# A decode block with attention over 65,536 keys: key and value chunks loaded in turn, a maximum for each chunk, one combination at the end

## The chip, the cores and the metric

The kernel runs on one core of one Trainium2 chip. The metric is the device time of one execution in microseconds (us), given as the median of several runs, with the lowest and the highest. Shorter is better. The profile is of one execution; where the record gives both, its span is about 1.8 us shorter than the time of the same run.

The engines are called as the profile calls them: PE is TensorE (matmuls), PEld its weight loads, DVE is VectorE, ACT is ScalarE, POOL is GpSimd, SP is SyncE, which here issues the loads. A load is one large transfer from memory into a buffer on the chip. The profile counts 16 DMA engines, and each load of the two kernels has 16 marks of completion.

## The reference, cut to what matters

One token goes through a block of a transformer. Attention has one query, 32 heads, 4 key/value heads of 65,536 keys with 128 elements each. All inputs are bfloat16.

```python
mod = (silu(c) @ w_mod).reshape(..., 6, 1, 1024)      # 1024 x 6144 weights: shifts, scales, gates
h = layernorm(x) * (1 + ca) + sa
q = h @ wq                                            # 1024 x 4096
p = softmax(q @ k.T * 128 ** -0.5)                    # k_cache: 4 x 65536 x 128, 8 query heads each
o = p @ v                                             # v_cache: the same shape
x = x + ga * (o @ wo)                                 # 4096 x 1024
h = layernorm(x) * (1 + cb) + sb
x = x + gb * ((gelu(h @ w_gate) * (h @ w_up)) @ w_down)   # 1024 x 3584 twice, 3584 x 1024
```

Everything is read once: 185.6 MB, of which 134 MB are keys and values. There is little arithmetic for each byte (the loads of the kernel before take 95.1% of the DMA engines' time, and PE is busy for 67% of the span), so the aim is that the loads never pause.

## The kernel before

All loads go through a ring of nine 2 MB buffers. SP issues a load as soon as the buffer that it goes to has been released by the matmuls that read it. The order of the loads is fixed by a schedule. `("A", g, cc)` is chunk cc of the keys of head group g, `("B", g, cc)` is a chunk of its values. A chunk has 8,192 keys, and a group has 8 chunks.

```python
NBUF = 9
SKEW = 7
...
S = min(SKEW, NCH)                       # NCH = 8 chunks in a group
for cc in range(NCH):
    sched.append(("A", 0, cc))
for g in range(Hkv):
    if g + 1 < Hkv:
        for cc in range(NCH):
            sched.append(("A", g + 1, cc))
            if cc >= S:
                sched.append(("B", g, cc - S))
        for cc in range(NCH - S, NCH):
            sched.append(("B", g, cc))
    else:
        for cc in range(NCH):
            sched.append(("B", g, cc))
```

With `SKEW = 7` this is eight key chunks of a group, then the eight value chunks of the group before, and so on: long runs of one kind. The two kinds differ in their cost. A key chunk is turned by 64 PE transposes into PSUM, copied out in four pieces of 128 x 2048 (three by DVE, 1.22 us each, one by ACT, 1.88 us), multiplied with the query in 64 matmuls, copied out as scores by ACT and reduced to a maximum by DVE. A value chunk costs only 64 matmuls (1.8 us; 128 take 3.58). The exponentials of a group wait for the maximum of the whole group:

```python
def emit_score_consume(g, cc):           # one key chunk
    ...
    dst = s_hm[:, :, cc * CH:(cc + 1) * CH].rearrange("p h n -> p n h")
    ... act.activation(dst, src, ACT.Copy, scale=scale)               # scores: PSUM -> SBUF
    ... dve.tensor_reduce(m_parts[:, :, cc:cc + 1], src3, AX.X, ALU.max)

def emit_group_max_and_exp(g):           # once for eight key chunks
    ... dve.tensor_reduce(m_col[:, :], m_parts[:, :, :], AX.X, ALU.max)
    ...                                  # transpose, reduce, broadcast by PE and DVE
    for h in range(REP):
        ... act.activation(pb[:, h, :], s_hm[:, h, :], ACT.Exp,
                           bias=Mneg[:, hq:hq + 1], accum_out=z_col[:, hq:hq + 1])
```

The matrix-vector products of the weight stages start a new sum for every load and add the partial sums on DVE. The weights of gate and up are read with a step of 56 bytes between elements (`"p k (m b) -> p k b m", b=28`):

```python
ins = pe.matmul(pp[:, jl:jl + 1], jb.view[:, kk, jl * P:(jl + 1) * P],
                rhs_col[:, k0 + kk:k0 + kk + 1], start=(kk == 0), stop=(kk == nk - 1))
...
vd = C_DVE.bump(dve.tensor_tensor(dst, dst, pp[:, 0:nj], ALU.add))
```

Of the kernel before, what the change touches and what calls it, by code (L numbers as in the profile page):

```python
# [3 lines left out]
dt = mybir.dt  # L4
ACT = mybir.ActivationFunctionType
ALU = mybir.AluOpType
AX = mybir.AxisListType

P = 128
SLOT = 8192  # L10
NBUF = 9
CH_MAX = 64
SKEW = 7
# [3 lines left out]
NKT_BANKS = 16  # L17
DMA_ENGINES = ("sync",)


class Ctr:

    def __init__(self, nc, name):
        self.sem = nc.alloc_semaphore(name)
        self.n = 0

    def bump(self, ins, by=1):
        ins.then_inc(self.sem, by)
        self.n += by
        return self.n  # L30


class PoolBuf:
    def __init__(self, pool, view, fill_sem, fill_val, rel_sem):
        self.pool = pool
        self.view = view
        self.fill_sem = fill_sem
        self.fill_val = fill_val
        self.rel_sem = rel_sem

    def wait(self, eng):
        eng.wait_ge(self.fill_sem, self.fill_val)

    def release(self):
        self.pool.pending.append(self.rel_sem)


class Pool:

    def __init__(self, nc, engines, nbuf, elems):  # L50
        self.nc = nc
        self.engines = engines
        self.nbuf = nbuf
        self.bufs = [nc.alloc_sbuf_tensor(f"pool{i}", [P, elems], dt.bfloat16) for i in range(nbuf)]
        self.fill = [nc.alloc_semaphore(f"pfill{i}") for i in range(nbuf)]
        self.rel = [nc.alloc_semaphore(f"prel{i}") for i in range(nbuf)]
        self.nfill = [0] * nbuf
        self.njobs = 0
        self.pending = []

    def load(self, src, view_fn):
        slot = self.njobs % self.nbuf
        eng = self.engines[self.njobs % len(self.engines)]
        self.njobs += 1
        if self.nfill[slot] > 0:
            eng.wait_ge(self.rel[slot], self.nfill[slot])
        view = view_fn(self.bufs[slot][:, :])
        eng.dma_start(view, src).then_inc(self.fill[slot], 16)  # L68
        self.nfill[slot] += 1
        return PoolBuf(self, view, self.fill[slot], 16 * self.nfill[slot], self.rel[slot])  # L70


def bass_adaLN_cond__gqa_block_cached__geglu_ffn__decode_kernel(
# [15 lines left out]
    assert D % P == 0  # L89
# [7 lines left out]
    assert REP * Hkv == HQ and Hkv >= 2  # L97
    F = B_w_gate.shape[1]
    assert F % P == 0
    FD = F // P  # L100
    M6 = w_mod.shape[1]
    assert M6 == 6 * D
    MD = M6 // P
    NKPP = SK // P
    assert NKPP * P == SK
    CH = min(CH_MAX, NKPP)
    assert NKPP % CH == 0 and CH % 8 == 0
    NCH = NKPP // CH
    NTB = CH // 8
    assert SLOT % DH == 0 and CH * DH <= SLOT  # L110
    HW = SLOT // 2
    assert KD % 2 == 0
    assert REP * CH <= 512
    scale = float(DH) ** -0.5
    S = min(SKEW, NCH)

    sp = nc.sync
    pe = nc.tensor
    act = nc.scalar
    dve = nc.vector  # L120
    pool = nc.gpsimd
    dma_engines = [{"sync": nc.sync, "gpsimd": nc.gpsimd, "scalar": nc.scalar}[e] for e in DMA_ENGINES]

    C_PE = Ctr(nc, "c_pe")
    C_DVE = Ctr(nc, "c_dve")
    C_ACT = Ctr(nc, "c_act")
    C_POOL = Ctr(nc, "c_pool")
# [3 lines left out]
    ident = nc.alloc_sbuf_tensor("ident", [P, P], dt.bfloat16)  # L131
    identf = nc.alloc_sbuf_tensor("identf", [P, P], dt.float32)
    onesf = nc.alloc_sbuf_tensor("onesf", [P, P], dt.float32)
    eps_t = nc.alloc_sbuf_tensor("eps_t", [P, 1], dt.float32)
    halfneg = nc.alloc_sbuf_tensor("halfneg", [P, 1], dt.float32)
    x_row = nc.alloc_sbuf_tensor("x_row", [KD, P], dt.bfloat16)
    c_row = nc.alloc_sbuf_tensor("c_row", [KD, P], dt.bfloat16)
    x_col = nc.alloc_sbuf_tensor("x_col", [P, KD], dt.float32)
    sg_col = nc.alloc_sbuf_tensor("sg_col", [P, KD], dt.float32)
    th_col = nc.alloc_sbuf_tensor("th_col", [P, KD], dt.float32)  # L140
    s_col = nc.alloc_sbuf_tensor("s_col", [P, KD], dt.bfloat16)
    mod_sb = nc.alloc_sbuf_tensor("mod_sb", [P, MD], dt.float32)
    q_acc = nc.alloc_sbuf_tensor("q_acc", [P, HQ], dt.float32)
    q_col = nc.alloc_sbuf_tensor("q_col", [P, HQ], dt.bfloat16)
    stats = nc.alloc_sbuf_tensor("stats", [P, 2], dt.float32)
    junk8 = nc.alloc_sbuf_tensor("junk8", [P, KD], dt.float32)
    me2 = nc.alloc_sbuf_tensor("me2", [P, 2], dt.float32)
    msq = nc.alloc_sbuf_tensor("msq", [P, 1], dt.float32)
    var = nc.alloc_sbuf_tensor("var", [P, 1], dt.float32)
    std1 = nc.alloc_sbuf_tensor("std1", [P, 1], dt.float32)  # L150
    rstd = nc.alloc_sbuf_tensor("rstd", [P, 1], dt.float32)
    hn = nc.alloc_sbuf_tensor("hn", [P, KD], dt.float32)
    ht = nc.alloc_sbuf_tensor("ht", [P, KD], dt.float32)
    h_col = nc.alloc_sbuf_tensor("h_col", [P, KD], dt.bfloat16)
    stats2 = nc.alloc_sbuf_tensor("stats2", [P, 2], dt.float32)
    junk8b = nc.alloc_sbuf_tensor("junk8b", [P, KD], dt.float32)
    me22 = nc.alloc_sbuf_tensor("me22", [P, 2], dt.float32)
    msq2 = nc.alloc_sbuf_tensor("msq2", [P, 1], dt.float32)
    var2 = nc.alloc_sbuf_tensor("var2", [P, 1], dt.float32)
    std2 = nc.alloc_sbuf_tensor("std2", [P, 1], dt.float32)  # L160
    rstd2 = nc.alloc_sbuf_tensor("rstd2", [P, 1], dt.float32)
    attn_acc = nc.alloc_sbuf_tensor("attn_acc", [P, KD], dt.float32)
    x1_col = nc.alloc_sbuf_tensor("x1_col", [P, KD], dt.float32)
    t_att = nc.alloc_sbuf_tensor("t_att", [P, KD], dt.float32)
    hn2 = nc.alloc_sbuf_tensor("hn2", [P, KD], dt.float32)
    ht2 = nc.alloc_sbuf_tensor("ht2", [P, KD], dt.float32)
    h2_col = nc.alloc_sbuf_tensor("h2_col", [P, KD], dt.bfloat16)
    kt_sb = nc.alloc_sbuf_tensor("kt_sb", [P, NKT_BANKS, 8, DH], dt.bfloat16)
    s_hm = nc.alloc_sbuf_tensor("s_hm", [P, REP, NKPP], dt.float32)
    p_hm = nc.alloc_sbuf_tensor("p_hm", [P, REP, NKPP], dt.bfloat16)  # L170
    m_parts = nc.alloc_sbuf_tensor("m_parts", [P, REP, NCH], dt.float32)
    m_col = nc.alloc_sbuf_tensor("m_col", [P, REP], dt.float32)
    z_col = nc.alloc_sbuf_tensor("z_col", [P, HQ], dt.float32)
    mg8 = nc.alloc_sbuf_tensor("mg8", [REP, 1], dt.float32)
    md8 = nc.alloc_sbuf_tensor("md8", [REP, REP], dt.float32)
    Mneg = nc.alloc_sbuf_tensor("Mneg", [P, HQ], dt.float32)
    rz = nc.alloc_sbuf_tensor("rz", [P, REP], dt.float32)
    o_sb = nc.alloc_sbuf_tensor("o_sb", [P, HQ], dt.bfloat16)
    o_pk = nc.alloc_sbuf_tensor("o_pk", [P, HQ], dt.bfloat16)
    QW = P // HQ  # L180
    assert QW * HQ == P and HQ == DH // QW
    LPAD = P - QW
    Lext = nc.alloc_sbuf_tensor("Lext", [P, P + LPAD], dt.bfloat16)
    Mmod = nc.alloc_sbuf_tensor("Mmod", [P, HQ], dt.bfloat16)
    Rmat = nc.alloc_sbuf_tensor("Rmat", [P, HQ, HQ], dt.bfloat16)
    g_acc = nc.alloc_sbuf_tensor("g_acc", [P, FD], dt.float32)
    u_acc = nc.alloc_sbuf_tensor("u_acc", [P, FD], dt.float32)
    t1 = nc.alloc_sbuf_tensor("t1", [P, FD], dt.float32)
    t2 = nc.alloc_sbuf_tensor("t2", [P, FD], dt.float32)
    t3 = nc.alloc_sbuf_tensor("t3", [P, FD], dt.float32)  # L190
    th = nc.alloc_sbuf_tensor("th", [P, FD], dt.float32)
    t4 = nc.alloc_sbuf_tensor("t4", [P, FD], dt.float32)
    u_col = nc.alloc_sbuf_tensor("u_col", [P, FD], dt.bfloat16)
    dn_acc = nc.alloc_sbuf_tensor("dn_acc", [P, KD], dt.float32)
    t_dn = nc.alloc_sbuf_tensor("t_dn", [P, KD], dt.float32)
    y_col = nc.alloc_sbuf_tensor("y_col", [P, KD], dt.float32)
    y_row = nc.alloc_sbuf_tensor("y_row", [KD, P], dt.bfloat16)

    kt_ps = nc.alloc_psum_tensor("kt_ps", [P, 4 * 1024], dt.bfloat16)
    sc_ps = nc.alloc_psum_tensor("sc_ps", [P, 2 * 512], dt.float32)  # L200
    b6 = nc.alloc_psum_tensor("b6", [P, 512], dt.float32)
    b7 = nc.alloc_psum_tensor("b7", [P, 512], dt.float32)
    PP = [sc_ps[:, 0:512], sc_ps[:, 512:1024]]

    B6_CT, B6_XT, B6_TOT, B6_MBC, B6_TOT2 = 0, 8, 16, 128, 144
    B7_OT, B7_ZBC, B7_PK = 0, HQ, 64
    assert HQ + REP <= 64 and B7_PK + max(HQ, FD) <= 512
    kt_fp = kt_ps[:, :].bitcast(dt.float32)
    KT4 = [kt_fp[:, i * 512:(i + 1) * 512] for i in range(4)]
# [3 lines left out]
    def peI(ins, bump=False):  # L213
        if bump:
            return C_PE.bump(ins)
# [601 lines left out]
```

## Time and profile before

| | before |
|---|---|
| time, median of 3 | 466.35 us (466.33 to 467.19) |
| span of the profiled execution | 467.1 us |
| share of 16 DMA engines' time taken by the loads | 95.1% |
| best rate of a slice | 434 GB/s |
| lowest slices inside the stream | 324, 333 and 307 GB/s |

The page divides the span into 40 slices of 11.7 us. These are its rows for PE and DMA busy time (in tenths; 9 is 90% or more) and for the bytes moved, and its lines of the DMA queues (packets, MB, share of the time of 16 engines).

```profile
PE   1344378778687785668877847778785545649963
...
DMA  7999999999999989999998899999789999999992
GB/s 303 422 425 427 430 432 428 426 427 428 428 431 429 406 324 425 429 429 429 421 366 333 348 429 428 431 429 365 307 331 406 434 428 425 422 421 423 430 430 98
...
q1 hardware_dynamic: 15856, 185.61, 95.1%
q8 instruction: 61, 1.00, 0.8%
```

Queue 1 carries the loads. The rate is 420 to 434 GB/s wherever nothing disturbs it, but there are three dips, the deepest slices of which lie near 170, 250 and 335 us (the 15th, 22nd and 29th slice). No slice of this page is above 434 GB/s. (Windows of 10 us read up to 438; a packet counts whole in the window in which it starts.) So the kernel is bound by its loads, and what can be gained is the dips and the two ends. Queue 8 has 61 packets of 16 KB each that the kernel's code does not ask for: they are fetches of the kernel's own instructions.

The dips come from the order of the loads. The timeline of PE in a run of key chunks, in three steps of the cycle (start us, us, line and operation, count, and in brackets the idle time before and what ended it; L506 are transposes, L549 scores):

```profile
107.26 1.95 PE L506 MATMUL kt_ps<-ident,pool 128*128 128x128 bf16 x32
110.59 2.20 PE L506 MATMUL kt_ps<-ident,pool 128*128 128x128 bf16 x32 [1.38 <-DVE kt_sb L531]
112.63 1.74 PE L549 MATMUL sc_ps<-q_col,kt_sb 128*128 128x8 bf16 x64
114.23 1.95 PE L506 MATMUL kt_ps<-ident,pool 128*128 128x128 bf16 x32
```

A key chunk takes 6.97 us (from 107.26 to 114.23), with PE held up by the copies out of PSUM (`kt_sb`, L531). A 2 MB load takes 4.9 us at the full rate. So PE falls behind by 2 us in each key chunk, sixteen of them in a row at the start (groups 0 and 1) and eight in each later run. In the end the nine buffers are full, and SP has no free buffer to load into (its longest wait for one is 11.0 us). These are PE's two costliest waits of the whole kernel (line, cause, total us, number, longest):

```profile
PE b L626 <- issue: 40.3, 14, 6.1
PE kt_ps L506 <- DVE kt_sb L531: 36.9, 31, 1.6
```

The second is the copies. The first belongs to the runs of values, in which PE is quicker than the loads.

```profile
384.97 3.58 PE L626 MATMUL b<-p_hm,pool 128*128 128x8 bf16 x128 [2.02 <-issue]
391.17 3.58 PE L626 MATMUL b<-p_hm,pool 128*128 128x8 bf16 x128 [2.61 <-issue]
397.36 2.73 PE L626 MATMUL b<-p_hm,pool 128*128 128x8 bf16 x96 [2.61 <-issue]
```

These matmuls come in blocks of 128 every 6.2 us, with idle time before each that the profile puts down to "issue": PE waited for nothing that the profile shows. The loads went on at 420 GB/s and more here, so it cost nothing in this last run. Two earlier runs of values (174 to 197 and 260 to 285 us) show the same stops, 8.1 and 11.2 us in all, although every value that they read had landed before they began. There they kept PE from making up its lag before the next run of keys, and so probably deepened the second and third dip; no run tests that.

### The profile page before, as it was taken

The numbers are of one execution on the slowest core, as the hardware profiler recorded it, in microseconds if no ns is written. First come the engines' busy times: TensorE is split into PE (matmuls) and PEld (weight loads), VectorE is DVE, ScalarE is ACT, GpSimd is POOL, SyncE is SP. The second block draws the span as 40 slices with busy tenths as digits, with TensorE's granted clock in tenths as the row PEclk, the third lists the DMA queues.
The fourth block names the chain that finished last, engine by engine and source line by source line (L and its number), as shares of the span: only waits on it lengthen the run. The fifth ranks groups of instructions, "written<-read, shape, count | busy, mean of one in ns | idle before, by whom it ended". The sixth has DMA issues, their size and how long they took to land.

```text
span 467.1 us, 16270 instructions
## 1 busy us (share of the span) xinstructions
PE 314.2 (67%) x7771; PEld 299.3 (64%) x7771; DVE 149.2 (32%) x204; ACT 115.1 (25%) x131; POOL 3.8 (1%) x22
## 2 busy tenths in 40 slices
PE   1344378778687785668877847778785545649963
PEld 1334377767686785668867747668685445649962
DVE  0001055665556550045575103455640000110010
ACT  1000014334463440027434200744350040000000
POOL 2000000000000000000000000000000000000000
PEclk9999999999799995568999756899985555555555
DMA  7999999999999989999998899999789999999992
GB/s 303 422 425 427 430 432 428 426 427 428 428 431 429 406 324 425 429 429 429 421 366 333 348 429 428 431 429 365 307 331 406 434 428 425 422 421 423 430 430 98
DMA packets 15922, 186.65 MB, mean 400 GB/s; under 512 B 1520, under 2 KB 1520, under 8 KB 4592
## 3 DMA queue, kind: packets, MB, share of 16 engines
q1 hardware_dynamic: 15856, 185.61, 95.1%
q8 instruction: 61, 1.00, 0.8%
q14 instruction: 5, 0.04, 0.0%
HBM read 185.60 MB, written 0.00 MB: 397 GB/s over the span
## 4 chain that ended last, share of the span: by engine, by line
issue 81%; DMA 13%; PE 3%; SPq 2%; DVE 1%; POOLq 0%; POOL 0%
DMA pool<-in_B_w_down_dram 7%; DMA pool<-in_w_mod_dram 6%; PE kt_ps L417 2%; SPq L68 1%; PE kt_ps L399 0%; PE sc_ps L348 0%; PE b L438 0%; POOLq L782 0%; POOL rstd L450 0%; PE b L774 0%; SPq L251 0%; DVE hn L453 0%; DVE y_row L776 0%; SPq L252 0%; DVE dn_acc L388 0%
## 5 line engine op out<-in xcount | busy, mean ns | idle before, releaser
L506 PE MATMUL kt_ps<-ident,pool 128*128 128x128 bf16 x2048 | 140.9, 229 | 43.8 <-DVE kt_sb L531 36.9
L506 PEld LDWEIGHTS kt_ps<-ident,pool 128*128 128x128 bf16 x2048 | 126.4, 104 | 54.0 <-DVE kt_sb L531 47.4
L531 DVE COPY kt_sb<-kt_ps 128x2048 bf16<-128x2048 bf16 x96 | 114.5, 1218 | 19.6 <-PE kt_ps L506 18.7
L529 ACT ACTIVATE kt_sb<-kt_ps 128x2048 bf16<-128x2048 bf16 x32 | 60.1, 1877 | 228.5 <-PE kt_ps L506 228.5
L626 PE MATMUL b<-p_hm,pool 128*128 128x8 bf16 x2048 | 57.3, 175 | 40.3 <-issue 40.3
L626 PEld LDWEIGHTS b<-p_hm,pool 128*128 128x128 bf16 x2048 | 56.0, 102 | 41.4 <-issue 41.3
L549 PE MATMUL sc_ps<-q_col,kt_sb 128*128 128x8 bf16 x2048 | 55.7, 166 | 0.0
L549 PEld LDWEIGHTS sc_ps<-q_col,kt_sb 128*128 128x128 bf16 x2048 | 54.5, 96 | 0.0
L574 DVE TENSOR_REDUCE m_parts<-s_hm 128x8 f32<-128x512 f32 x32 | 22.0, 688 | 87.1 <-ACT s_hm L570 87.1
L570 ACT ACTIVATE s_hm<-sc_ps 128x512 f32<-128x512 f32 x32 | 33.7, 1054 | 0.4 <-PE sc_ps L549 0.4
L606 ACT ACTIVATE p_hm<-s_hm,Mneg 128x512 bf16<-128x512 f32 x32 | 22.6, 708 | 32.2 <-DVE Mneg L595 32.2
L651 DVE RECIPROCAL rz<-b 128x8 f32<-128x8 f32 x4 | 0.8, 208 | 93.0 <-PE b L647 93.0
L417 PE MATMUL kt_ps<-h_col,pool 128*128 128x1 bf16 x448 | 28.7, 202 | 2.6 <-DVE h_col L462 2.2
L417 PEld LDWEIGHTS kt_ps<-h_col,pool 128*128 128x128 bf16 x448 | 28.5, 167 | 2.7 <-DVE h_col L462 2.3
L348 PE MATMUL sc_ps<-s_col,pool 128*128 128x1 bf16 x384 | 11.4, 165 | 21.0 <-DMA pool<-in_w_mod_dram 21.0
L348 PEld LDWEIGHTS sc_ps<-s_col,pool 128*128 128x128 bf16 x384 | 10.9, 104 | 21.5 <-issue 18.8
L759 ACT ACTIVATE th<-t 128x28 f32<-128x28 f32 x1 | 0.2, 225 | 71.1 <-DVE t L757 71.1
L348 PE MATMUL sc_ps<-h_col,pool 128*128 128x1 bf16 x256 | 7.4, 165 | 12.0 <-DMA pool<-in_A_wq_dram 12.0
L348 PEld LDWEIGHTS sc_ps<-h_col,pool 128*128 128x128 bf16 x256 | 7.2, 104 | 12.2 <-issue 9.3
L399 PE MATMUL kt_ps<-u_col,pool 128*128 128x1 bf16 x224 | 6.6, 165 | 8.9 <-DMA pool<-in_B_w_down_dram 7.2
L399 PEld LDWEIGHTS kt_ps<-u_col,pool 128*128 128x128 bf16 x224 | 6.3, 104 | 9.3 <-DMA pool<-in_B_w_down_dram 7.5
L399 PE MATMUL kt_ps<-o_pk,pool 128*128 128x1 bf16 x256 | 7.3, 165 | 4.9 <-issue 4.6
(79 smaller groups left out, 49.3 us busy)
## 6 DMA issues: line engine op xcount, KB each, us to landing
pool<-in_A_k_cache_dram SPq DMA_DIRECT2D x32, 2048.0 KB, 24.3
pool<-in_A_v_cache_dram SPq DMA_DIRECT2D x32, 2048.0 KB, 13.2
pool<-in_w_mod_dram SPq DMA_DIRECT2D x4, 2048.0 KB, 17.7
pool<-in_A_wq_dram SPq DMA_DIRECT2D x4, 2048.0 KB, 28.6
pool<-in_A_wo_dram SPq DMA_DIRECT2D x4, 2048.0 KB, 21.6
pool<-in_B_w_gate_dram SPq DMA_DIRECT2D x4, 1792.0 KB, 27.8
pool<-in_B_w_up_dram SPq DMA_DIRECT2D x4, 1792.0 KB, 29.0
pool<-in_B_w_down_dram SPq DMA_DIRECT2D x3, 2048.0 KB, 31.0
```

Of the source, the lines that this page charges most:

```text
L68: eng.dma_start(view, src).then_inc(self.fill[slot], 16)
L348: ins = pe.matmul(pp[:, jl:jl + 1], jb.view[:, kk, jl * P:(jl + 1) * P], rhs_col[:, k0 + kk:k0 + kk + 1], start=(kk == 0), stop=(kk == nk ...
L399: ins = pe.matmul(pp[:, jl:jl + 1], jb.view[:, kk, jl * P:(jl + 1) * P], rhs_col[:, k0 + kk:k0 + kk + 1], start=(kk == 0), stop=(kk == nk ...
L417: ins = pe.matmul(pp[:, b:b + 1], jb.view.rearrange("p k (m b) -> p k b m", b=nb)[:, kk, b, :], rhs_col[:, k0 + kk:k0 + kk + 1], start=(kk ...
L506: ins = pe.transpose(kt_ps[:, phys * 1024 + i * P:phys * 1024 + (i + 1) * P], kb.view[:, n, :], ident[:, :],)
L529: ve = ctr.bump(act.activation(dst, src, ACT.Copy))
L531: ve = ctr.bump(dve.tensor_copy(dst, src))
L549: ins = pe.matmul(sc_ps[:, sbank * 512 + n * REP:sbank * 512 + (n + 1) * REP], kt_sb[:, tb % NKT_BANKS, i, :], q_col[:, g * REP:(g + 1) * ...
L570: state["sc_done"][gc] = C_ACT.bump(act.activation(dst, src, ACT.Copy, scale=scale))
L574: dve.tensor_reduce(m_parts[:, :, cc:cc + 1], src3, AX.X, ALU.max)
L606: act.activation(pb[:, h, :], s_hm[:, h, :], ACT.Exp, bias=Mneg[:, hq:hq + 1], accum_out=z_col[:, hq:hq + 1],)
L626: ins = pe.matmul(b7[:, B7_OT + g * REP:B7_OT + (g + 1) * REP], vb.view[:, n, :], pb[:, :, ncol], start=(cc == 0 and n == 0), stop=(cc == ...
```

## The change

The intent is a steady mixture: one step takes one key chunk and one value chunk, so that PE's work for a step is below the 10 us that its two loads take. That needs the exponentials of a chunk soon after its scores, so each chunk gets a maximum of its own, and the partial outputs, each relative to its own maximum, are kept apart in PSUM columns and weighted once at the end. Along with it, the scores go from PSUM straight into the exponential, matrix-vector products accumulate in PSUM, gate and up are read with a step of 8 bytes, and the removed score buffer makes room for a tenth slot. (The kernel before does not build with ten buffers: it asks for 16,384 bytes more in each partition with 224 left.)

```diff
-NBUF = 9
-SKEW = 7
+NSLOT = 10
+UE = 4
 ... order of the loads
-        for (kind, g, cc) in sched:
-            if kind == "A":
-                jobs_k[(g, cc)] = pool_ring.load(kh[g][:, cc * CH:(cc + 1) * CH, :], view_kv)
-            else:
-                jobs_v[(g, cc)] = pool_ring.load(vh[g][:, cc * CH:(cc + 1) * CH, :], view_kv)
+        for i in range(NC + 2):                        # NC = 32 chunks in all
+            if i < NC:
+                j_k[i] = plan_load(kv_src(kh, i), kv_view)
+            if i >= 2:
+                j_v[i - 2] = plan_load(kv_src(vh, i - 2), kv_view)
 ... exponentials of one chunk, straight from PSUM
+            for h in range(REP):
+                v = AC.done(act.activation(
+                        p_sb[:, i % 3, :, h], scv[:, h, :], ACT.Exp,
+                        bias=mneg[:, i, h:h + 1], scale=scale, accum_out=z_all[:, i, h:h + 1]))
 ... values: every chunk has its own columns
-                    b7[:, B7_OT + g * REP:B7_OT + (g + 1) * REP], vb.view[:, n, :], pb[:, :, ncol],
-                    start=(cc == 0 and n == 0), stop=(cc == NCH - 1 and n == CH - 1),
+                    b7[:, i * REP:(i + 1) * REP], j_v[i].view[:, n, :], p_sb[:, i % 3, n, :],
+                    start=(n == 0), stop=(n == CH - 1),
 ... one step: T transposes, QK scores, PV values (in quarters), MX1/MT/MB the maximum
+        for i in range(NC + 2):
+            on(T, i, 0); on(QK, i - 1, 0); on(T, i, 1); on(QK, i - 1, 1); on(PV, i - 2, 0)
+            on(T, i, 2); on(QK, i - 1, 2); on(QK, i - 1, 3); on(MX1, i - 1); on(PV, i - 2, 1)
+            on(T, i, 3); on(PV, i - 2, 2); on(MT, i - 1); on(PV, i - 2, 3); on(MB, i - 1)
 ... matrix-vector products: only the very first matmul of a bank starts a sum
-                            start=(kk == 0), stop=(kk == nk - 1),
+                            start=first, stop=True, skip_group_check=True,
                         )
+                        first = False
 ... the end: weights of the chunks, exp(own maximum to the group's), applied to sums and outputs
+        v_w = AC.done(act.activation(w_all[:, :, :], dw[:, :, :], ACT.Exp))
+        ... z_all * w_all, summed; b7 * w_all, summed; divided; packed for wo
```

The change relies on a single `start` for a whole bank. How the chip handles that no trace shows; that the sums come out right is shown: e4, e5 and e10, which keep this, are recorded as correct on the chip. Smaller parts of the change are not shown: `w_mod` comes in eight loads of 1.5 MB, the last 1 MB of `w_down` in two loads, and the inputs `x` and `c` are loaded from ACT instead of SP.

## The prediction

> **What bounds the kernel now.** The DMA engines. The page's slices show DMA at 0.9 or more in most slices and 425 to 434 GB/s when undisturbed; the page moves 185.6 MB of queue-1 data. One engine moves a 16 KB packet about every 607 ns (packet records), so 16 engines give 432 GB/s, 430 us for all of it. [...] The other 37 us of the 467 us span are, by my reading:
> - about 20 us of DMA dips: three dips in the slices, 324, 333 and 307 GB/s at about 175, 260 and 345 us. They come at the end of each run of eight K chunks: a K chunk takes TensorE 7.0 us (timeline: transposes gated by the 1.22 us VectorE evictions and the 1.88 us ScalarE one), while its DMA takes 4.9 us. Nine buffers do not cover that. In runs of V chunks TensorE needs 1.75 us of each 4.9 and idles.
> - about 3 us of ramp, and the end: bandwidth falls from 457 us, one engine finishes its last packets until 463.0, then 4.1 us of matmuls, VectorE, output.
> - uneven engines: between the first and the last of a load's 16 completion marks the gap grows to 4.7 us while streaming (0.6 at the start), shrinks after each dip, and is 6.2 us at the end.
>
> **What the change does.** K and V alternate, so one step consumes 4.19 MB, 9.8 to 10.0 us of DMA. TensorE work per step, from durations of before at full clock: 64 transposes at 56 ns 3.6, scores 1.74, PV 1.74, small matmuls with waits 1.0: about 8.1 us, under the DMA. VectorE: 3 x 1.22 + 0.7 + 0.45, 4.8 us. [...] The 1.05 us score copy goes. The step is DMA-bound, and the ten buffers are consumed in load order, so the three dips should vanish: about 20 us off the critical path. Off it: matvec accumulation in PSUM, and gate/up weight loads at 8-byte instead of 56-byte steps (64 ns a matmul now, 28 where contiguous). End: 16 matmuls instead of 32 after the last load and no reduction, minus 0.8 us. Start: first load 0.8 us earlier. The final combination (about 4 us) hides under the 20 us loading of wo.
>
> Given back: without dips the slowest engine never catches up. Its loads come at 4.98 us per 2 MB when streaming, against 4.87 for the first engine. 8.6 + 87.5 x 4.98 + 3.3 = 448 us, plus 2 for imperfections: **450 us**, 80% range 444.5 to 459. Faster by over 2%: 0.85; within 2%: 0.12; slower: 0.03.
>
> **What would make it wrong.** The TensorE clock. [...] this trace switches between 0.5 and 1.0, and transposes take 93 ns at half, while scores stay at 27. Windows of only scores or PV went to half clock here (at 122, 177, 262, 347 us). [...] I expect mixed clocks, about 9.5 us.
>
> **Checks.** Slices: no DMA slice below 410 GB/s between the first and the last two. DMA queue waits: loads wait for releases as a matter of course. TensorE waits for K and V loads each step, not for VectorE. Timeline: step period 9.8 to 10.2 us. Last completion mark 8 to 13 us behind the first. Gate/up matmuls under 45 ns apart. If instead TensorE has no load waits and the clock reads 0.5 to 0.7, the clock risk came true.

The sum of the forecast is 8.6 + 435.8 (87.5 x 4.98) + 3.3 = 447.7 us, and the 2 us on top are an allowance. The kernel after shows that the 64-element exponentials start 0.29 us apart (272.44, 272.73, 273.02 and 273.31 us). An estimate from the trace before: transposes start 107 ns apart at a recorded clock of 0.5 (the 93 of the prediction is a mean over a rise, see the end), score and value matmuls 27, so 64 x 0.107 + 128 x 0.027 and the prediction's 1.0 for small matmuls give 11.3 us, more than the 10 us of a step's loads. So the clock stays the risk that the prediction calls it; the "about 9.5 us" there is PE's work for a step.

## The result, and the profile after

| | before | after |
|---|---|---|
| time, median of 4 each, same rounds | 466.77 us (466.33 to 467.58) | 455.75 us (455.48 to 456.06) |
| ratio | | 0.9752 (95%: 0.9726 to 0.9777), faster |
| span of the profiled execution | 467.1 us | 454.3 us |
| mean granted TensorE clock | 0.795 | 0.748 |

A ratio here is the mean time of one kernel's runs over that of the other's runs of the same rounds, so it isn't quite the ratio of the medians. The predicted 450.0 us was 5.75 us too low, and the measured time lies inside the range of 444.5 to 459.

The same rows of the page for the kernel after (a slice is 11.4 us):

```profile
PE   1333478989998999989898998979998985554434
...
DMA  8999999999999999999999999999999999999972
GB/s 331 429 421 421 430 420 431 418 428 423 421 424 428 423 421 431 421 423 427 423 427 423 426 421 428 423 423 428 418 428 423 426 421 427 413 419 416 419 324 108
...
q1 hardware_dynamic: 15328, 185.61, 97.0%
q8 instruction: 61, 1.00, 0.9%
```

The three dips are gone: between the first and the last two, no slice is below 413 GB/s. PE is near 90% busy in the attention stage, but it now waits for loads. Its costliest waits in that stage, as line, cause, total us, number and longest:

```profile
PE b L420 <- DMA slot<-in_A_v_cache_dram: 17.2, 16, 2.2
PE b L420 <- ACT p_sb L407: 5.7, 3, 3.0
PE kt_ps L350 <- DMA slot<-in_A_k_cache_dram: 3.5, 2, 3.0
```

L420 are the value matmuls, L350 the transposes. The long queue of waits for `kt_sb` copies (36.9 us before) is down to 0.5 us. The step of the attention loop can be read from the small matmul that closes each step (L395):

```profile
200.84 0.59 PE L395 MATMUL b<-negi,mg 8*128 8x8 f32 x2
...
211.83 0.59 PE L395 MATMUL b<-negi,mg 8*128 8x8 f32 x2
...
221.77 0.38 PE L395 MATMUL b<-negi,mg 8*128 8x8 f32 x2
```

Two steps took 20.93 us here; over the whole stage a load comes every 5.035 us, a step every 10.07 us. In the weight stage, the same gate and up matmuls before (first line, a step of 56 bytes) and after (second, 8 bytes):

```profile
434.18 14.33 PE L417 MATMUL kt_ps<-h_col,pool 128*128 128x1 bf16 x224 [0.41 <-DVE g_acc L388]
```

```profile
429.12 2.03 PE L278 MATMUL kt_ps<-h_col,slot 128*128 128x1 bf16 x56 [2.33 <-DMA slot<-in_B_w_up_dram]
```

This is 64 ns for each before and 36 ns after (predicted: under 45); but the second line also says why that gains nothing: PE sits idle before it, waiting for the next load.

Last, the ends of the chains that ended last, before and after (start us, us, what):

```profile
430.32 32.68 DMA pool<-in_B_w_down_dram
...
463.04 1.03 PE kt_ps L399 x32
```

```profile
426.01 24.83 DMA slot<-in_B_w_down_dram
...
450.89 0.60 PE kt_ps L278 x16
```

In both, the last load sets the end; after it come 4.1 us before (463.0 to 467.1) and 3.4 us after. The last load landed 12.1 us earlier in the new kernel: of that, the first packet of the first weight load started 0.8 us earlier (1.76 instead of 2.56 us), and the rest is the stream itself.

### The mark that the dips had hidden

Both kernels wait for 16 increments of a semaphore for each load. The trace has the time of each, the marks; they don't come together. I read each as one engine's end of its share: a 2 MB load of keys or values has 128 packets of 16 KB, so eight of 0.61 us for each of 16 engines, 4.9 us, and that is the pitch of the first marks (4.895 us in the attention stage of the kernel after). No record names an engine. For the last load of each kernel, in us after the first packet of the first weight load:

| | first mark | 8th | 9th | last mark | lag, last less first | fetch packets |
|---|---|---|---|---|---|---|
| before | 454.27 | 455.05 | 456.99 | 460.43 | 6.16 | 61 |
| after | 435.61 | 438.54 | 446.58 | 449.08 | 13.47 | 61 |

In the kernel after, eight engines were done by 438.5 and the other eight only from 446.6. I call them the early and the late half. For the early engines the change is worth 18.7 us (454.27 to 435.61), close to the "about 20 us" of dips in the prediction. For the late ones, which decide, it is 11.35 us. During a dip of the kernel before SP could issue no load; as I read it, the early engines ran dry and the late ones used that time to catch up. Without the dips they never do (e8 below shows a dip that did so). The prediction said so and put the lag at 8 to 13 us. It did not say what makes half of the engines late.

### The profile page after: what moved, and what is told of

It is laid out like the page before. It is cut to its first block, busy times and chain, and to the rows that moved or that the text cites. A ratio compares the mean times of both kernels' runs of the same rounds, so it can differ in the third digit from the quotient of the medians.

```text
span 454.3 us, 16671 instructions
## 1 busy us (share of the span) xinstructions
PE 347.1 (76%) x7849; PEld 336.6 (74%) x7849; DVE 161.7 (36%) x237; ACT 143.2 (32%) x548; POOL 3.7 (1%) x21
## 4 chain that ended last, share of the span: by engine, by line
DMA 80%; PE 15%; ACT 2%; SPq 1%; DVE 1%; issue 1%
DMA slot<-in_A_v_cache_dram 59%; DMA slot<-in_A_wq_dram 9%; DMA slot<-in_B_w_up_dram 7%; PE kt_ps L350 6%; DMA slot<-in_B_w_down_dram 5%; PE b L420 4%; PE sc_ps L371 2%; PE kt_ps L278 1%; SPq L182 1%; ACT p_sb L407 1%; PE sc_ps L278 0%; ACT kt_sb L362 0%; PE b L388 0%; PE b L395 0%; DVE Rmat L480 0%
## 5 line engine op out<-in xcount | busy, mean ns | idle before, releaser
L350 PE MATMUL kt_ps<-ident,slot 128*128 128x128 bf16 x2048 | 181.8, 260 | 5.8 <-DMA slot<-in_A_k_cache_dram 3.5
L350 PEld LDWEIGHTS kt_ps<-ident,slot 128*128 128x128 bf16 x2048 | 157.1, 119 | 9.0 <-DMA slot<-in_A_k_cache_dram 3.9
L362 DVE COPY kt_sb<-kt_ps 128x2048 bf16<-128x2048 bf16 x96 | 117.6, 1225 | 106.5 <-PE kt_ps L350 105.6
L420 PE MATMUL b<-p_sb,slot 128*128 128x8 bf16 x2048 | 72.3, 168 | 25.6 <-DMA slot<-in_A_v_cache_dram 17.2
L420 PEld LDWEIGHTS b<-p_sb,slot 128*128 128x128 bf16 x2048 | 66.4, 101 | 27.3 <-DMA slot<-in_A_v_cache_dram 18.8
L407 ACT ACTIVATE p_sb<-sc_ps,mneg 128x64 bf16<-128x64 f32 x256 | 83.7, 559 | 4.8 <-DVE mneg L401 4.7
L407 ACT ACTIVATION_READ_ACCUMULATOR p_sb<-sc_ps,mneg 128x1 f32 x256 | 77.2, 362 | 0.0
L278 PE MATMUL kt_ps<-h_col,slot 128*128 128x1 bf16 x448 | 16.2, 172 | 19.0 <-DMA slot<-in_B_w_up_dram 10.6
L278 PEld LDWEIGHTS kt_ps<-h_col,slot 128*128 128x128 bf16 x448 | 15.6, 118 | 19.7 <-DMA slot<-in_B_w_up_dram 10.9
L384 DVE TENSOR_REDUCE m_col<-sc_ps 128x8 f32<-128x512 f32 x32 | 21.8, 681 | 4.3 <-PE sc_ps L371 4.3
L278 PE MATMUL sc_ps<-h_col,slot 128*128 128x1 bf16 x256 | 7.4, 165 | 12.8 <-DMA slot<-in_A_wq_dram 12.8
L395 PE MATMUL b<-negi,mg 8*128 8x8 f32 x64 | 15.8, 318 | 0.4 <-DVE mg L390 0.4
L395 PEld LDWEIGHTS b<-negi,mg 8*128 8x128 f32 x64 | 12.8, 249 | 2.5 <-DVE mg L390 0.6
## 6 DMA issues: line engine op xcount, KB each, us to landing
slot<-in_B_w_up_dram SPq DMA_DIRECT2D x4, 1792.0 KB, 31.2
```

The lines of the kernel that those rows point to most:

```text
L278: ins = pe.matmul(bank[:, j:j + 1], w, rhs[:, k0 + kk:k0 + kk + 1], start=first, stop=True, skip_group_check=True,)
L350: ins = pe.transpose(kt_ps[:, half * 2048 + t * P:half * 2048 + (t + 1) * P], j_k[i].view[:, b * TB + t, :], ident[:, :],)
L362: ev[(i, b)] = E_.done(act.activation(dst, src, ACT.Copy) if E_ is AC else dve.tensor_copy(dst, src))
L384: mx[i] = DVE.done(dve.tensor_reduce(m_col[:, i % 2, :].unsqueeze(2), sc_view(i), AX.X, ALU.max))
L395: pe.matmul(b6[:, 256:256 + REP], mg8[:, i % 2:i % 2 + 1].to_broadcast([REP, P]), negi[:, :], start=True, stop=True,)
L407: act.activation(p_sb[:, i % 3, :, h], scv[:, h, :], ACT.Exp, bias=mneg[:, i, h:h + 1], scale=scale, accum_out=z_all[:, i, h:h + 1],)
```

## The experiments

The theories are these.

- **Order**: the gain comes from the order of the loads alone; the rest of the change is needed for nothing, or only for room. Its rivals: the tenth buffer, the cheaper matrix-vector products, or the maximum of each chunk carry a part.
- **Fetch**: half of the engines are late because they carry the fetches of the kernel's instructions, and that is what keeps the time above the pure stream. Rivals: the engines differ by nature, or TensorE at half clock and the waits for it cost the difference.
- **Supply**, which came up later (an expectation that speaks of theory E means it): while loads fill the DMA engines, instructions for TensorE arrive only at a limited rate, and a kernel that needs more of them is bound by that.

Kernels whose results are wrong are marked so. "Ratio" is against the kernel before in the same rounds, whose median was 467.18 in the first rounds, 466.82 in the second (466.81 in the third), and 466.39 us in the last.

### e1: the kernel before with one constant changed

```diff
-SKEW = 7
+SKEW = 1
```

Keys of a group and values of the group before now alternate, and nothing else changes: one maximum for a group, nine buffers, sums on DVE.

> The kernel before with one constant changed, the skew of its schedule from 7 chunks to 1, so that from the second head group on K and V chunks are loaded and used in turn; one maximum per head group, nine buffers and everything else stay. Theory A (the gain is the alternating order, which lets the K chunks' surplus of TensorE time be hidden under the V chunks' DMA): the three DMA dips go, 451 to 459 us, ratio 0.965 to 0.984, and the last completion mark lags the first by 10 to 14 us. Rival B (the gain needs the chunk maxima, the score copy's removal or the tenth buffer): 462 us or more, dips at the group boundaries.

Measured: 456.46, 454.81 and 453.41 us, and one run of 1,197.97 us, ratio 0.9737 (0.9685 to 0.9788). The profile fell on the slow run. Of that profile, the page's line of the engines' busy time (us, share of the span, instructions) and its DMA row, and then three groups of instructions (line, engine, operation, shapes, count, busy us, mean ns):

```profile
PE 1158.3 (97%) x7771; PEld 1073.8 (90%) x7771; DVE 154.4 (13%) x204; ACT 118.1 (10%) x131; POOL 3.8 (0%) x22
...
DMA  9995111123133333351333333331333333268760
```

```profile
L506 PE MATMUL kt_ps<-ident,pool 128*128 128x128 bf16 x2048 | 680.2, 705 | 0.5 <-DVE q_col L471 0.5
L506 PEld LDWEIGHTS kt_ps<-ident,pool 128*128 128x128 bf16 x2048 | 579.3, 314 | 76.8 <-DVE q_col L471 0.6
L549 PEld LDWEIGHTS sc_ps<-q_col,kt_sb 128*128 128x128 bf16 x2048 | 184.1, 215 | 4.0
```

A weight load took 215 to 314 ns instead of about 100, and a transpose 705 ns instead of 229, so PE was busy the whole time and the loads waited for it. DVE's copies were as always (1,225 ns). The recorded clock of this run was 1.0. A clock far below the recorded one would fit these durations (680.2 us for 2,048 transposes is 332 ns each, where those of the kernel before start 56 ns apart while its recorded clock is 1.0 and 107 ns apart while it is 0.5), but that is a guess, and one run can't tell more. The run is left out. The other three already say that the order alone is worth as much as the whole change; whether the dips had gone, they can't say without a profile. e8 repeats it.

### e2 and e3: nothing but the loads, without and with instructions to fetch

All computation of the kernel after is replaced. For each load in turn, PE waits for it, runs `DUMMY` matmuls on a constant and one matmul that reads the load, and releases it. The results are wrong; the order, sizes and number of the loads and buffers are those of the kernel after.

```diff
+        for j in list(loads):
+            PE.wait(j.tok)
+            for _i in range(DUMMY):                    # e2: 0, e3: 84
+                pe.matmul(b6[:, 0:REP], ident[:, :], ident[:, 0:REP], start=True, stop=True)
+            release(j, PE.done(pe.matmul(b6[:, 8:8 + REP], slots[j.slot][:, 0:P], ...)))
```

84 were chosen so that TensorE executes about as many instructions as in the kernel after (7,905 matmuls against 7,849).

> Wrong result on purpose: the changed kernel with all its loads, in the same order and through the same ten buffers, but each load is consumed by a single matmul; some 450 instructions instead of 16,671. Theory A (the span is the slowest DMA engine's, and what slows it is fetching the kernel's own instructions, 61 packets of 16 KB on half the engines): the lag between first and last completion mark stays under 3 us and the time is 441 to 445 us. Rival C (the engines differ by themselves, or the loads alone have a pitch of 5.04 us per 2 MB on the slowest engine): the lag still grows to 10 us or more and the time is 450 to 455 us.

> Wrong result on purpose: as the loads-only run, but 84 small matmuls on constants come before each load's one matmul, so that the instruction count is again near 16,500 while TensorE, VectorE and ScalarE have nothing to make the DMA wait for. Theory A (instruction fetch makes the lag): the lag returns to 11 to 14 us and the time is 453 to 456 us, within 2 us of the changed kernel. Rival C: same as the loads-only run. Rival D (TensorE at half clock costs the changed kernel the 5 us above its prediction): this run is 3 us or more faster than the changed kernel at 455.75.

Measured: e2 442.53 us (442.45 to 442.69), ratio 0.9473 (0.9431 to 0.9515). e3 458.50 us (458.28 to 458.59), ratio 0.9813 (0.9777 to 0.9849). Their page's lines, e2 first, then e3:

```profile
GB/s 322 432 423 425 427 428 428 428 428 428 428 430 428 428 428 428 431 428 428 428 428 428 428 428 428 428 428 428 428 428 428 428 428 428 421 421 420 418 423 291
...
q1 hardware_dynamic: 15328, 185.61, 99.5%
```

```profile
GB/s 333 426 422 417 425 429 421 428 425 426 425 422 431 421 428 422 428 425 426 422 426 429 419 428 426 423 426 426 425 423 429 419 431 416 420 415 417 418 267 64
...
q1 hardware_dynamic: 15328, 185.61, 96.4%
q8 instruction: 61, 1.00, 0.9%
```

e2 has no queue 8 line at all: its 332 instructions needed no packet of that queue. Its last slice is still at 291 GB/s and all 16 marks of its last load come within 0.97 us. e3 has the 61 packets, and its last two slices fall to 267 and 64, like those of the kernel after. Its marks (table below e10) are those of the kernel after within 0.7 us. So the engines are not different by nature (in e2 the first and the last mark both advance by 4.896 us for each load of 2 MB). And what the kernel after loses against the pure stream is, but for at most 0.7 us, not due to the TensorE clock or to waits for computation: a kernel with none of that computation ends its loads at nearly the same time. e3's time missed its expectation (453 to 456 us, within 2 us of the kernel after). It is 2.75 us above the kernel after since more matmuls are left at its end: its last three blocks of 84 run from 447.7 to 454.6 us of a span of 456.7.

### e9: half the instructions

As e3, with `DUMMY = 42`. If the fetches make the lag, it halves.

> Wrong result on purpose: the loads with 42 small matmuls each instead of 84, half the instructions. If the lag is in proportion to the instructions fetched: 31 fetch packets, a lag of 6 to 7.5 us, and a time halfway between the two earlier loads runs, 448 to 451 us (442.5 without, 458.5 with 84, of which about 3.5 us are the last load's own matmuls).

Measured: 449.48 us (449.4 to 449.5), ratio 0.9623 (0.9592 to 0.9655), wrong.

```profile
GB/s 333 426 421 421 427 427 426 425 429 427 423 430 427 426 425 427 429 423 429 427 425 429 427 426 422 433 426 425 430 425 423 426 430 427 415 418 418 419 419 134
...
q8 instruction: 31, 0.51, 0.5%
```

31 fetch packets and a lag of 7.00 us: in the middle.

### e6 and e10: more fetches in the kernel after

e6 was meant to add instructions on GpSimd, away from TensorE, so as to part the fetches from the matmuls that they are fetched for:

> The changed kernel, and 3,200 one-element memsets on the otherwise idle GpSimd (19% more instructions), started after the first normalisation and done well before GpSimd is next needed. Theory A (instruction fetch slows half the DMA engines): 12 more fetch packets, the lag grows from 13.5 to 15 to 17 us and the time by 1 to 3.5 us. Rival C (lag is not from fetching): lag and time unchanged within 0.7 us.

It was refused (a race in how the added memsets were ordered on GpSimd). e10 instead adds 50 matmuls on constants after each load of the weight stages but the last, 18% more TensorE instructions. Its results stay right.

```diff
                 release(jb, tok)
+                for _i in range(0 if jb is j_d[-1][0] else 50):
+                    pe.matmul(b7[:, 496:496 + REP], ident[:, :], ident[:, 0:REP], start=True, stop=True)
```

> The changed kernel, correct, with 50 small matmuls on constants after each of 28 weight loads, in stretches where TensorE waits for DMA anyway: 2,800 more instructions, 17%. If fetching sets the slow engines' pace: about 10 or 11 more fetch packets, the lag grows from 13.5 to 15 to 16.5 us and the time by 1.2 to 3.5 us over 455.75. If TensorE work or waits set the time instead: unchanged within 0.7 us.

Measured: 468.56 us (467.04 to 469.27), ratio 1.0028 (0.9993 to 1.0063): 12.8 us slower than the kernel after, where 1.2 to 3.5 had been expected. A clear miss. The marks did what the fetch theory says:

| kernel | fetch packets | TensorE instructions / 256 | first mark | last mark | lag | last mark over e2's, for each packet of one late engine |
|---|---|---|---|---|---|---|
| e2 | 0 | 0.7 | 435.72 | 436.69 | 0.97 | |
| e9 | 31 | 31.2 | 435.59 | 442.58 | 7.00 | 1.52 us |
| e3 | 61 | 61.8 | 435.54 | 448.39 | 12.85 | 1.53 us |
| after | 61 | 61.3 | 435.61 | 449.08 | 13.47 | 1.62 us |
| e10 | 72 | 72.3 | 435.51 | 449.97 | 14.47 | 1.48 us |

The third column counts matmuls and weight loads (7,849 of each in the kernel after), divided by 256: it matches the packets, so one packet of 16 KB holds 256 instructions of TensorE. The last column divides the delay of the last mark by the packets of one late engine, taken as an eighth of all; for e3, (448.39 - 436.69) / (61 / 8) = 1.53 us. It is nearly constant. The early half always ends at 435.5 to 435.7, with or without fetches. A fetch packet is recorded with 0.93 to 1.07 us (medians of the runs), against 0.61 us for a load's packet of 16 KB.

But the extra 12.8 us of e10 did not come from the lag. Its loads ended by 452 us of a 467.5 us span. The time went into PE, as the timeline of the weight stage shows; the first three lines are from the time when the loads still ran, the last two from when they had ended:

```profile
397.08 0.24 PE L286 MATMUL b<-ident 128*128 128x8 bf16 x3 [1.88 <-issue]
...
403.28 1.57 PE L278 MATMUL kt_ps<-o_pk,slot 128*128 128x1 bf16 x53 [2.62 <-issue]
...
409.48 1.20 PE L278 MATMUL kt_ps<-o_pk,slot 128*128 128x1 bf16 x39 [2.63 <-issue]
```

```profile
455.88 1.84 PE L278 MATMUL kt_ps<-u_col,slot 128*128 128x1 bf16 x64
457.59 1.53 PE L286 MATMUL b<-ident 128*128 128x8 bf16 x50
```

While the loads run, PE stops for 1.9 to 2.6 us every 6.2 us (before 397.08, 403.28 and 409.48), in the middle of a row of matmuls whose data is there, and the cause is "issue". Between two stops lie 128 matmuls with their weight loads: 256 instructions, one fetch packet. After the loads have ended, it runs on without a gap. This is the pattern of the value runs of the kernel before (384.97, 391.17, 397.36). It gave the theory of supply.

### e12: the supply limit by itself

As e3, with `DUMMY = 126`: 254 TensorE instructions for each load. Their matmuls take about 3.6 us for each load, less than the load itself.

> Wrong result on purpose: the loads with 126 small matmuls each, 1.5 times as many as in the run that reached the changed kernel's time. TensorE needs about 28 ns x 126, 3.5 us, of the 5 us that a load takes, so by its busy time it is not the limit. Theory E (while the DMA engines are full, TensorE is handed its instructions in blocks of 256, at most one block per 6.1 us, as the gaps without a wait in the run with 17% more instructions suggest): one block a load, a load every 6 us, a time of 530 to 575 us, and such gaps throughout. Lag theory alone (92 fetch packets slow eight engines, nothing else): 462 to 470 us.

Measured: 536.1 us (536.0 to 536.2, 2 runs), ratio 1.1498 (1.1464 to 1.1532), wrong. The wait list of PE, and its timeline while the loads run and after they have ended:

```profile
PE b L259 <- issue: 193.0, 84, 3.7
PE b L259 <- DMA slot<-in_w_mod_dram: 7.4, 1, 7.4
```

```profile
301.61 3.09 PE L259 MATMUL b<-ident 128*128 128x8 bf16 x110 [2.08 <-issue]
...
307.53 3.07 PE L259 MATMUL b<-ident 128*128 128x8 bf16 x109 [2.35 <-issue]
...
313.73 3.04 PE L259 MATMUL b<-ident 128*128 128x8 bf16 x108 [2.62 <-issue]
```

```profile
521.45 3.56 PE L259 MATMUL b<-ident 128*128 128x8 bf16 x126
```

PE waited 193 us for "issue" in 84 places, and only once for a load. The first 25 packets follow each other at 6.1 us on average; with idle DMA engines, 126 matmuls follow at once in 3.56 us. The loads themselves ran at 420 GB/s or more for the first 160 us, in which the ten buffers took up the difference (5 us for a load, 6.1 for its instructions), and at 320 to 405 after that, since PE released the buffers late. The theory of supply expected 530 to 575 us, the lag alone 462 to 470. The limit is shown for a stream of loads with small matmuls; that the fetch waits behind queued load packets in the DMA engines is the obvious reading, and is argued, not shown. Here the lag of the last load was 0.65 us in spite of 92 fetches, which fits the holes in its stream, in which late engines can catch up.

### e8: e1 again

> The kernel of the skew run again, unchanged, because the profile of that run fell on one execution of 1198 us in which every TensorE instruction was slow. Theory A (the alternating order alone removes the three dips): 453 to 457 us, no DMA slice under 405 GB/s between the second and the third last, final completion marks 11 to 14 us apart. If the dips were still there and the gain came from elsewhere, slices near 330 to 370 GB/s would show it.

Measured: 455.40 us (453.11 to 457.91) in five fast runs, ratio 0.9756 (0.9717 to 0.9795). A sixth of 461.63 us, over 1.5% above the fastest, is left out. The profile has a span of 455.1 us and this row:

```profile
GB/s 299 424 423 426 431 432 428 429 426 428 431 429 425 429 429 427 428 429 428 428 429 422 392 425 428 431 369 426 423 419 419 428 275 402 419 426 424 431 428 162
...
q8 instruction: 61, 1.00, 0.8%
```

So the order alone gives the whole gain. The expectation that no slice falls below 405 failed: three shorter dips are left (392, 369, 275), and the lag was 3.04 us, not 11 to 14. The marks explain it. The early half ended at 445.07, 9.5 us later than in the kernel after; the last mark came at 448.11, 1 us earlier. A dip shorter than the lag cost nothing: from 298 us to 306 us the early engines' first marks were 8.2 us apart instead of 4.9, while the last marks of the same loads were 4.84 us apart, no more than elsewhere. As I read it, the late engines still had packets queued when the early ones ran dry. The dip from 371 to 381 us held both, by 10.2 and 8.95 us, and so was paid for in part. The spread of e8's fast runs is 4.8 us against 0.6 us in the kernel after; what makes it vary was not looked into.

### e4 and e5: two parts of the change undone

e4 reads gate and up at 56 bytes again (`-UE = 4`, `+UE = 28`, with `w_down` cut to suit). e5 has nine slots (`-NSLOT = 10`, `+NSLOT = 9`).

> The changed kernel with the gate and up weights read again at steps of 56 bytes instead of 8. Theory A (off the critical path): the gate and up matmuls go from 35 to 64 ns apart, 3.6 us per load instead of 2.0, still under the 4.36 us that a load's DMA takes, and the time stays within 1 us of 455.75. Rival: if TensorE bounds the last stage, 448 matmuls x 29 ns, 13 us slower at most.

> The changed kernel with nine load buffers, as the kernel before has, instead of ten. Theory A (alternating loads are consumed as they come, so the tenth buffer matters little): within 1.5 us of 455.75, no DMA dips. Rival B (the tenth buffer carries the gain): dips return, 460 us or more.

Measured: e4 455.32 us (455.16 to 455.77), ratio 0.9747 (0.9711 to 0.9784); e5 455.49 us (455.4 to 455.57), ratio 0.9758 (0.9721 to 0.9795). Neither differs from the kernel after (0.9752). Both parts are off the critical path. The outputs are right.

### e7, e11 and e13: last loads that avoid the late engines

If the last loads could go to the early engines alone, the estimate was that up to 13 us, the lag, would be free. In these traces each piece of 8, 6 or 4 partitions has 9, 7 or 5 marks instead of 16, one of them right at its issue; I read the others as 8, 6 and 4 engines. (The output of the kernel after, over 8 partitions, looks the same: issued from 452.66 us on, one mark at 453.14, eight from 453.79 to 453.87.) e7 cuts the last two loads of 0.5 MB into loads of 8 partitions each, e11 the last one into loads of 6, e13 into loads of 4, always through SP:

```diff
+                jb.cuts = [(p, min(p + 4, P)) for p in range(0, P, 4)] if e == UE - 2 else None
 ...
+                for p0, p1 in j.cuts:
+                    sp.dma_start(j.view[p0:p1, :, :], j.src[p0:p1, :, :]).then_inc(j.tok[0], 16)
```

Which engines a piece uses no trace shows. An assumption: "the lower eight" are the eight that a piece of 8 partitions uses, and "numbered 6 and 7" are the two of them that a piece of 6 would leave out. By the marks of the kernel after, the last load of 0.5 MB puts 1.26 us on an engine (from the load before it to this one, the first marks advance from 434.35 to 435.61), half of what was reckoned with.

> The changed kernel with its last two loads, 0.5 MB each, cut into sixteen loads of 8 partitions each. [...] Theory A (eight engines fetch instructions and end 11 to 13.5 us behind the other eight): if the lower eight are the fast ones, [...]the time falls by 3 to 5 us to about 451.5; if the lower eight are the slow ones, it rises by 3 to 5 us, which would tell which half it is. Rival (the lag is spread otherwise): change within 1.5 us.

> The changed kernel with only its last 0.5 MB load cut into 6-partition loads[...]. The 8-partition cut was slower by 6 us, and its marks showed two late engines among those that it used. If these two are numbered 6 and 7: [...]the time falls by 1.5 to 2.5 us to about 453.7. If one or both are below 6: it rises by 2 to 6 us.

> The changed kernel with its last 0.5 MB load cut into 4-partition loads[...]. If all four are among the early ones: [...]the time falls by 1.5 to 2.5 us to about 453.5, which would beat both kernels. If a late one is among them: it rises by 5 us or more.

Measured: e7 461.92 us (460.88 to 462.62), ratio 0.9893 (0.9865 to 0.9922). e11 459.16 us (458.19 to 459.87), ratio 0.9833 (0.9802 to 0.9863). e13 456.86 us (456.52 to 457.07), ratio 0.9799 (0.9776 to 0.9822). All lose: by the medians, 6.2, 3.4 and 1.1 us against the kernel after; e7 lost more than the 3 to 5 us expected. In e7 and e11 the cut loads ended last, on engines that are among the late ones. No record names an engine, but the marks of the last load count them. In e7, 32 marks of its 16 pieces came from 452.5 us on, when all others had come by 446.6: two of eight engines are late. In e11, 21 came from 448.9 on: one of six. In e13 all had come by 446.5, while the uncut loads' late marks came up to 450.6: none of four. e13 fits neither of its two expectations, and its chain shows why:

```profile
416.95 32.44 DMA slot<-in_B_w_down_dram
...
449.43 2.73 PE kt_ps L285 x96
```

The cut load was no longer the last. The wait that ended last was that for the last uncut 2 MB load, at 449.38 us, and then 96 matmuls of 2.73 us remained, where the kernel after had 16 of 0.60 us after its last load at 450.85. Both uncut loads at the end landed about 1 us later than in the kernel after (449.38 and 450.64 us against 448.34 and 449.59), so the last landing moved forward by 0.2 us only, and the later matmuls gave back more. Why these two came later was not looked into. Little was to be had from the last load alone, as the late engines still owe their share of the loads before it. No version with right results beat both kernels by more than the scatter.

## Why the prediction was right or wrong

- **The loads bound the kernel, and the dips are what the change removes**: right. 95.1% of the engines' time became 97.0%, and no slice fell below 413 (predicted: none below 410).
- **"About 20 us off the critical path", given back by the slowest engine**: right in its mechanism. The early engines gained 18.7 us, the late ones, which decide, 11.35 us.
- **The term that was mis-sized**: "Its loads come at 4.98 us per 2 MB when streaming", 87.5 times. In the attention stage of the kernel after, the late engines took 5.035 us for each load (342.37 us for 68), and counted as the prediction counts, from its 8.6 us to the last mark at 450.85, it was 5.054 us on average. So the term came to 442.3 us instead of 435.8, 6.5 us more, enough for the whole miss of 5.75. The other terms hardly moved: the end took 3.4 us for 3.3, and the "2 for imperfections" happened to match the 1.8 us between span and time of the same run (454.3 and 456.06 us for the kernel after), which the prediction did not name; that is luck. Of the 0.055 us in the attention stage, a part is in the early engines too, which took 4.895 us for each load (as all engines do in e2) against the 4.87 of the prediction. Another part is that the 4.98 fits a stretch of the kernel before (about 40 to 165 us) with 0.64 fetch packets for each load, against 0.73 in the attention stage of the kernel after; at 1.53 us for each packet of one of eight engines that is an estimate of 0.02 us. The rest is not resolved. What e2, e9 and e3 show is that the late engines' pace is not a constant of the chip: it grew with the number of instructions run for each load (4.896, 4.965 and 5.034 us in e2, e9 and e3), so it can't be carried from one stretch of work to another.
- **The lag "8 to 13 us"**: 13.47, just outside.
- **The clock as the main risk**: it did turn out mixed (0.748, predicted mixed), and PE needed nearly the whole step, but it cost at most 0.7 us: e3, without any of the computation and with a recorded clock of 1.0, ended its loads only that much earlier. (The 93 ns of the prediction is a mean over a stretch in which the clock rose, 64 transposes in 5.96 us; at a recorded clock of 0.5 the trace has 107 ns.) The records of the kernel before show what came before the clock's changes: each of the six rises to 1.0 came after 3.4 us that held 26 to 32 transposes and at most two other matmuls, and two of the falls to 0.5 (at 176.8 and 262.2 us) after 3.4 us of about 130 score and value matmuls of 8 columns, 25 to 27 ns apart, so PE had not been idle. What sets the clock no run tests. The prediction's "TensorE waits for K and V loads each step" was too strong: 16 waits for values and 2 for keys in 32 steps. "Not for VectorE" held (0.5 us).
- **Step of 9.8 to 10.2 us, gate and up under 45 ns, first load 0.8 us earlier, end 0.8 us shorter, combination hidden under the loads of wo**: 10.07 us, 36 ns, 0.8 us, 0.7 us (4.1 to 3.4), and 414 GB/s while the combination ran (386 to 390 us). Right.
- **What the prediction did not see**: that the changed order is the only part that counts. One constant in the kernel before gives the same time (e1, e8). The maximum of each chunk, the tenth slot, the accumulation in PSUM and the 8-byte step together gain nothing here; only the slot and the step were also undone one at a time. And the step of the new loop is near another limit: in its attention stage a fetch packet comes every 6.56 us on average (7.03 in the kernel before), where e12, with its loads at 420 GB/s or more, got one every 6.1 us. A key chunk is 128 matmuls with their weight loads, 256 instructions. So, as an estimate from e12's 6.1 us, a run of keys alone would lag behind its loads (4.9 us) even if the copies, which made it 6.97 us, cost nothing; no run tests that. e10 shows what comes behind it.

What stays open: whether the fetch packets alone slow the late engines or the matmuls' own reads take part, since a matmul is always fetched too (that the early half never moved, and that the delay is the same 1.5 us for each packet, speaks for the packets); which eight engines are the late ones, beyond what the cut loads tell; the run of 1,198 us; the scatter of e8.

## What to carry to other kernels

When a kernel is bound by its loads, mix the work so that each stretch of loads has less compute than load time, and look first for the constant that sets the order, before rewriting anything. Judge a removed dip by the slowest engine's completion marks, not by the mean rate: in e8 a dip shorter than the engines' lag was free, and a longer one was paid for in part. Count TensorE instructions for each load: here, at one packet per 256 of them, they delayed half of the engines by about 1.5 us for each packet of one engine (e2, e3, e9, e10), and in e12, with the loads at 420 GB/s or more, one packet came every 6.1 us.
